# Gated attention plus MLP on one core: row-tiled scores, column-tiled PV on moving exponentials, a share of the exponentials on VectorE, and a list-scheduled engine order

## The chip, the cores and the metric

The kernel runs on one NeuronCore of one Trainium2 chip. The metric is the device time of one execution in microseconds (us). Each run is fast or slow (slow: more than 1.5% above the fastest of the same kernel); comparisons below use fast runs. The engines are named as in the profile: PE (TensorE matmuls), PEld (its weight loads), DVE (VectorE), ACT (ScalarE), POOL (GpSimd), SP (SyncE).

A profile is one execution taken by the hardware profiler. The trace behind it lists every instruction with its start and duration.

## The reference, cut to what matters

```python
def _A_ref(x, wqkv, wo):                       # x: 1 x 2048 x 640, bf16
    H = 32; Dh = 20
    qkv = (x @ wqkv) ...                       # q, k, v: 32 heads of 20 columns
    scores = einsum("bhqd,bhkd->bhqk", q, k) * Dh ** -0.5
    p = softmax(scores)                        # 32 x 2048 x 2048 exponentials
    o = einsum("bhqk,bhkd->bhqd", p, v)
    return o.reshape(B, S, D) @ wo

def _B_ref(x, w1, b1, w2):                     # F = 1536
    h = x @ w1 + b1
    act = h * tanh(softplus(h))                # mish
    return act @ w2

g = sigmoid((x * gate_w).sum(-1, keepdims=True))
return g * _A_ref(x, ...) + (1 - g) * _B_ref(x, ...)
```

The head dimension of 20 shapes everything: a score matmul uses 20 of the 128 rows of the PE array (in the trace its form is 20\*128, that of a projection 128\*128), and a PV product has only 21 useful columns (20 of V and a column of ones that sums the exponentials). The 134 million exponentials are the other large load.

## The kernel before

For each chunk of 512 queries and each group of two heads the kernel goes over 16 tiles of 128 keys. Two score matmuls fill a tile of 1024 columns in PSUM, ACT makes the exponentials, and eight matmuls with the *exponentials as weights* and V as the moving operand accumulate the output. Projections and MLP work are pumped in between on a credit count.

```python
for j in range(NS):                                   # 16 key tiles
    Sp = aps.tile([P, 2 * QC], F32, tag="S")
    for t in range(2):                                # two heads, two row strips
        nc.tensor.matmul(Sp[:, QC*t : QC*(t+1)],
            lhsT=kT_all[base+ROWB*t : base+ROWB*t+DH, p, j*P:(j+1)*P],
            rhs=qTc_p[base+ROWB*t : base+ROWB*t+DH, 0:QC],
            tile_position=(base + ROWB * t, 0))
    E = e_pool.tile([P, 2 * QC], BF16, tag="E")
    nc.scalar.activation(E, Sp, ACT.Exp, scale=inv_sqrt_dh)
    for t in range(2):
        for u in range(NU):                           # four blocks of 128 queries
            nc.tensor.matmul(acc[:, u, t, 0:DH+1],
                lhsT=E[:, QC*t + P*u : QC*t + P*(u+1)],   # exponentials as weights
                rhs=VA[:, j, h, 0:DH+1], ...)             # 21 moving columns
    pump_slot(slot_credit)                            # projections or MLP work
```

[... projections, mish by the identity (e^2+2e)/(e^2+2e+2) with a DVE reciprocal, output projection, and a transposing DMA of x at the start are cut ...]

The softmax here doesn't subtract the row's maximum and nothing guards it: scores larger than these inputs give would overflow.

## Time and profile before

| | before |
|---|---|
| time | 1387.95 us, median of 2 (1376.44 to 1399.46, the second 1.7% above the first and so slow by the rule above) |
| PE busy | 1235.3 us, 89% of the span |
| ACT busy | 1053.3 us, 76% |
| DVE busy | 463.9 us, 34% |
| mean granted PE clock | 0.608 of full |

The page's busy table, its slices (each digit is a fortieth of the span, in tenths busy; PEclk is the granted clock in tenths), and its chain of work that ended last:

```profile
PE 1235.3 (89%) x12384; PEld 589.6 (43%) x12384; DVE 463.9 (34%) x1093; ACT 1053.3 (76%) x1138; POOL 28.6 (2%) x51
...
PE   0699999988999988998889998998889988998887
...
ACT  0286666987768877698998777698998787699995
...
PEclk9975555975585555795555555695555555695555
...
PE 67%; ACT 25%; issue 3%; DMA 3%; DVE 1%; ACTq 0%
```

PE is nearly full while its clock is mostly at half, and the chain is two thirds PE.

Groups of instructions, by shape (out<-in, count | busy us, mean ns of one | idle just before them and what ended it):

```profile
L406 ACT ACTIVATE E<-Sp 128x1024 bf16<-128x1024 f32 x1024 | 1006.0, 1022 | 223.6 <-PE Sp L395 213.0 <-PE acc L412 0.9 <-ACT E L406 0.5
L395 PE MATMUL Sp<-qTc_p,kT_all 20*128 20x512 bf16 x2048 | 589.2, 559 | 0.0
L412 PE MATMUL acc<-VA,E 128*128 128x21 bf16 x8192 | 398.1, 182 | 95.5 <-ACT E L406 93.5 <-DVE O_qc L423 0.3
L412 PEld LDWEIGHTS <-E 128*128 128x128 bf16 x8192 | 335.7, 106 | 471.1 <-ACT E L406 376.9 <-issue 58.2 <-ACT e_sb L231 17.0
```

ACT lost 213.0 us waiting for scores. The 8192 small PV matmuls keep PE busy for 398.1 us and stream only 21 columns each.

### The profile page before, as it was taken

How to read it: one execution, taken by the hardware profiler on the slowest of the kernel's cores; microseconds unless marked ns; L12 is line 12 of the kernel's file. 1: busy time of each engine (PE TensorE's matmuls, PEld its weight loads, DVE VectorE, ACT ScalarE, POOL GpSimd, SP SyncE). 2: the span in 40 equal slices, each digit the busy share in tenths (PEclk: the TensorE clock that was granted, in tenths of full speed). 3: DMA queues.
4: the chain of work that ended last, by engine and by line, in shares of the span. 5: the costliest groups of instructions: out<-in, count | busy, mean ns of one | idle time of the engine just before them, and what ended most of it. 6: DMA issues, size and time to landing. Idle time of an engine off the chain costs nothing.

```text
span 1383.0 us, 28359 instructions
## 1 busy us (share of the span) xinstructions
PE 1235.3 (89%) x12384; PEld 589.6 (43%) x12384; DVE 463.9 (34%) x1093; ACT 1053.3 (76%) x1138; POOL 28.6 (2%) x51
## 2 busy tenths in 40 slices
PE   0699999988999988998889998998889988998887
PEld 0354444544444444443434444443434444453333
DVE  0222222377722576410101477410001476510002
ACT  0286666987768877698998777698998787699995
POOL 7000000000000000000000000000000000000000
PEclk9975555975585555795555555695555555695555
DMA  9600000000000000000000000000000000000000
GB/s 185 109 8 7 8 7 7 2 1 1 13 8 11 11 1 1 1 21 1 1 1 11 11 1 1 1 2 1 1 2 6 16 2 1 1 2 1 1 1 20
DMA packets 53086, 16.91 MB, mean 12 GB/s; under 512 B 49408, under 2 KB 52096, under 8 KB 52960
## 3 DMA queue, kind: packets, MB, share of 16 engines
q1 hardware_dynamic: 47456, 9.30, 4.6%
q0 software_dynamic: 912, 4.75, 1.2%
q10 hardware_dynamic: 4592, 1.03, 0.6%
q8 instruction: 97, 1.59, 0.5%
q14 instruction: 29, 0.24, 0.1%
HBM read 7.21 MB, written 2.62 MB: 7 GB/s over the span
## 4 chain that ended last, share of the span: by engine, by line
PE 67%; ACT 25%; issue 3%; DMA 3%; DVE 1%; ACTq 0%
PE Sp L395 26%; ACT E L406 25%; PE acc L412 15%; PE ph L223 8%; PE pk L143 5%; PE pb L261 4%; DMA xT<-in_A_x_dram 3%; PE pq L208 3%; PE pa L304 3%; PE pv L186 3%; PE pt L288 1%; ACTq L406 0%; PE pv L171 0%; ACT e_sb L231 0%; DVE d L311 0%
## 5 line engine op out<-in xcount | busy, mean ns | idle before, releaser
L406 ACT ACTIVATE E<-Sp 128x1024 bf16<-128x1024 f32 x1024 | 1006.0, 1022 | 223.6 <-PE Sp L395 213.0
L395 PE MATMUL Sp<-qTc_p,kT_all 20*128 20x512 bf16 x2048 | 589.2, 559 | 0.0
L412 PEld LDWEIGHTS <-E 128*128 128x128 bf16 x8192 | 335.7, 106 | 471.1 <-ACT E L406 376.9
L412 PE MATMUL acc<-VA,E 128*128 128x21 bf16 x8192 | 398.1, 182 | 95.5 <-ACT E L406 93.5
L241 DVE RECIPROCAL rd<-rd 128x256 f32<-128x256 f32 x96 | 167.4, 1744 | 0.8
L395 PEld LDWEIGHTS <-kT_all 20*128 20x128 bf16 x2048 | 104.3, 98 | 51.5 <-issue 18.2
L223 PE MATMUL ph<-xTc,w_sb 128*128 128x256 bf16 x480 | 119.0, 403 | 0.1
L421 DVE RECIPROCAL rden<-acc 128x8 f32<-128x8 f32 x64 | 12.4, 193 | 297.4 <-PE acc L412 297.4
L223 PEld LDWEIGHTS <-w_sb 128*128 128x128 bf16 x480 | 51.7, 128 | 57.4 <-issue 42.6
L234 DVE SCALAR_TENSOR_TENSOR e_sb<-e_sb 128x256 f32<-128x256 f32 x96 | 40.4, 421 | 100.5 <-ACT e_sb L231 99.6
L215 DVE CAST qTc_p<-pq 128x512 bf16<-128x512 f32 x32 | 22.1, 691 | 148.8 <-PE Sp L395 98.6
L231 ACT ACTIVATE e_sb<-ph,b1f 128x256 f32<-128x256 f32 x96 | 45.4, 473 | 33.8 <-PE ph L223 29.9
L143 PE MATMUL pk<-xT,wk 128*128 128x512 bf16 x140 | 66.0, 548 | 0.0
L208 PE MATMUL pq<-xTc,wqp 128*128 128x512 bf16 x160 | 64.5, 492 | 0.0
L261 PE MATMUL pb<-w_sb,actT 128*128 128x512 bf16 x192 | 58.0, 419 | 0.1
L150 DVE CAST kT_all<-pk 128x512 bf16<-128x512 f32 x32 | 22.1, 691 | 96.3 <-PE pk L143 96.3
L186 PE MATMUL pv<-wv,xT 128*128 128x80 bf16 x560 | 50.7, 237 | 0.0
L193 DVE CAST VA<-pv 128x80 bf16<-128x80 f32 x128 | 30.4, 243 | 57.7 <-PE pv L186 51.5
L143 PE MATMUL pk<-xT,wk_118 128*128 128x512 bf16 x20 | 7.2, 544 | 44.4 <-DMA xT<-in_A_x_dram 44.4
L243 DVE SCALAR_TENSOR_TENSOR actT<-ph,b1f,rd 128x256 bf16<-128x256 f32 x96 | 45.8, 478 | 0.1
L186 PEld LDWEIGHTS <-xT 128*128 128x128 bf16 x560 | 33.4, 117 | 23.2 <-issue 23.0
L261 PEld LDWEIGHTS <-actT 128*128 128x128 bf16 x384 | 28.5, 101 | 33.3 <-issue 24.1
(101 smaller groups left out, 351.9 us busy)
## 6 DMA issues: line engine op xcount, KB each, us to landing
w_sb<-in_B_w_dram POOLq DMA_DIRECT2D x2, 1920.0 KB, 31.1
out_dram<-ot SPq DMA_DIRECT2D x16, 160.0 KB, 1.8
Wq<-in_A_wqkv_dram ACTq DMA_DIRECT2D x1, 800.0 KB, 4.9
wo_sb<-in_A_wo_dram POOLq DMA_DIRECT2D x1, 800.0 KB, 24.5
wv<-in_A_wqkv_dram SPq DMA_DIRECT2D x7, 100.0 KB, 2.3
wk<-in_A_wqkv_dram SPq DMA_DIRECT2D x28, 25.0 KB, 2.6
wv_114<-in_A_wqkv_dram ACTq DMA_DIRECT2D x1, 100.0 KB, 10.7
wk_118<-in_A_wqkv_dram ACTq DMA_DIRECT2D x4, 25.0 KB, 29.7
```

The costliest lines, as they stand in the source:

```text
L143: nc.tensor.matmul(pk[:, 0:QC], lhsT=wk[:, kt, 0:P], rhs=xT[:, kt, sc * QC : (sc + 1) * QC], start=(kt == 0), stop=(kt == KT - 1),)
L186: nc.tensor.matmul(pv[:, 0 : 4 * DH], lhsT=lhsT, rhs=wv[:, kt, :], start=(kt == 0), stop=(kt == KT - 1),)
L208: nc.tensor.matmul(pq[:, 0:QC], lhsT=wqp[:, kt, p, 0:P], rhs=xTc[:, kt, 0:QC], start=(kt == 0), stop=(kt == KT - 1),)
L223: nc.tensor.matmul(ph[:, 0:CH], lhsT=w1_sb[:, kt, ft * P : (ft + 1) * P], rhs=xTc[:, kt, half * CH : (half + 1) * CH], start=(kt == 0), st ...
L231: nc.scalar.activation(e_sb, ph[:, 0:CH], ACT.Exp, bias=b1f[:, ft : ft + 1], scale=1.0)
L241: nc.vector.reciprocal(out=rd, in_=rd)
L243: nc.vector.scalar_tensor_tensor(out=actT[:, ft, half * CH : (half + 1) * CH], in0=ph[:, 0:CH], scalar=b1f[:, ft : ft + 1], in1=rd, op0=AL ...
L261: nc.tensor.matmul(tile_[:, 0 : col1 - col0], lhsT=actT[:, ft, u * P : (u + 1) * P], rhs=w2_sb[:, ft, col0:col1], start=(ft == 0), stop=(f ...
L304: nc.tensor.matmul(pa[:, :], lhsT=oT[:, ct, u * P : (u + 1) * P], rhs=wo_sb[:, ct, 0:CB], start=(ct == 0), stop=(ct == KT - 1),)
L395: nc.tensor.matmul(Sp[:, QC * t : QC * (t + 1)], lhsT=kT_all[base + ROWB * t : base + ROWB * t + DH, p, j * P : (j + 1) * P,], rhs=qTc_p[b ...
L406: nc.scalar.activation(E[:, :], Sp[:, :], ACT.Exp, scale=inv_sqrt_dh)
L412: nc.tensor.matmul(acc[:, u, t, 0 : DH + 1], lhsT=E[:, QC * t + P * u : QC * t + P * (u + 1)], rhs=VA[:, j, h, 0 : DH + 1], start=first, s ...
```

## The change

The intent has four parts. Scores: four heads of a group in four 32-row strips, two or three issued side by side. PV: V (with its ones column) becomes the *weights*, 32 columns wide, and the exponentials *move*, 512 at a time; four heads sit in four column strips of the array, so that one key tile of four heads is one bundle. Exponentials: for key tiles 6, 10 and 14 DVE makes them by bit fields, so ACT has 13 of 16. Order: every operation becomes a task with a cost, and a list scheduler written into the kernel fixes the order of each engine at build time. Mish moves to ACT (Exp, Ln, Tanh), x is transposed on PE, not by DMA, and the softmax normaliser goes through DRAM to be broadcast over partitions.

```diff
+DVE_KEYS = (6, 10, 14)
+ACT_KEYS = tuple(j for j in range(NS) if j not in DVE_KEYS)
+COEF = (0.458054, 0.465699, 0.0762946)
+SCALE = 0.5 / COEF[1]
+COEF = tuple(SCALE * c for c in COEF)
[...]
+class Order:                       # list scheduler: pick, for each engine, the task that
+    ...                            # can start first, by priority; for PE with look-ahead
[...]
+    for a, (G, j, r) in enumerate(blk):          # 3 or 2 blocks, by turns
+        nc.tensor.matmul(sb.tile[:, a*QC:(a+1)*QC],
+            lhsT=kt_all[32*r:32*r+32, G % NP, j*P:(j+1)*P],
+            rhs=q_buf[G].tile[32*r:32*r+32, :],
+            start=True, stop=True, tile_position=(32*r, 0))
+    nc.scalar.activation(eb.tile[:, 0:w], sb.tile[:, 0:w], ACT.Exp, bias=lnc, scale=inv)
[...]
+    for r in range(4):                           # PV: one bundle
+        ten, off = v_ap(j, 4*p + r, term)
+        nc.tensor.matmul(acc[32*r:32*r+32, :], lhsT=ten[:, off:off+32], rhs=srcs[r](),
+            start=k == 0, stop=k == pv_per - 1, tile_position=(0, 32*r))
[...]
+    # DVE's share: score * 128/ln2 + 127*128 written as uint16 is 2^n(1+f) as bf16 bits (e);
+    # n = e & 0xFF80;  m = (e & 0x7F) | 0x3F80;  m = m*m;  m = m*e
+    # the exponential is COEF[0]*n + COEF[1]*e + COEF[2]*m: three PV bundles with scaled V
+    nc.vector.tensor_scalar(out=e, in0=db.tile, scalar1=P*LOG2E*inv, scalar2=127.0*P,
+                            op0=ALU.mult, op1=ALU.add)
[...]
-    for j in range(NS):                          # the loop shown above, and the credit pump
[... 1259 lines of diff in all ...]
```

The bias `lnc` is the logarithm of SCALE. It scales ACT's exponentials so that COEF[1] can be exactly one half.

## The prediction

> **What bounds the kernel now.** TensorE, because its clock is low. The page's busy table has PE at 1235.3 us (89%), ACT 1053.3 (76%), DVE 463.9 (34%); the chain of waits is 67% PE, 25% ACT; the waits view has ACT idle 213.0 us for scores. The cores view gives a mean granted clock of 0.608. I replayed the matmul records in windows of 3.41 us and summed columns x rows/128 against the full-clock capacity. Of all windows that kept or won the full clock none used under 0.37, and those that lost it used 0.36 or less. Attention alone uses about 0.12 to 0.33 of the array, so the clock falls to half. [...] this trace shows only 1.0 and 0.5, in stretches of multiples of that.
>
> **What changes.**
> - Scores: still 2048 matmuls of 512 columns, but two or three 32-row strips at once, not two.
> - PV: 8192 matmuls of 21 columns (398.1 us busy, waiting 93.5 us for exponentials) and their 335.7 us of weight loads become 2816 of 512 columns, four column strips at once, with 32-column weights: 704 bundles of about 0.22 us at full clock (512-column durations less overlap), 0.43 at half.
> - ACT: 2048 blocks of 512 exponentials become 1664, in tiles of 1536 and 1024. Back to back, 128x1024 took 0.97 us in the timeline; from that and the slope I estimate 1.40 for 1536. 333 pairs: 789 us. Mish adds 36 activations of 2048 (estimate 1.82 each: 66 us) and 25 table loads at 1.283 (32 us). ACT about 890 us.
> - DVE takes 3 of 16 key tiles: 384 PSUM reads of 512 columns (0.691 each, as the casts now: 265 us), 192 bit-field passes and 384 multiplies of estimated 0.69 (forms scaled from 0.286, 0.419, 0.424 us): about 400 us. With evacuations 820 to 870 us. The mish reciprocal (167.4 us) and its companions go.
> - The DMA transposes go; PE now waits 44.4 us for the first. First exponential about 18 us after the start.
>
> **What then binds.** ACT first (890), DVE close (850), PE at full clock about 750 with switches between tilings. Per group of heads each needs 24 to 27 us. Weighted array use of the whole kernel is 1.17 M columns, 490 us at full clock: 0.5 of a 980 us span, above the 0.37 line, so I expect mean clock 0.80 to 0.95. In stretches without projections or MLP (about six of 32 groups, the last 2.6 above all) use is about 0.33, so the half clock returns and scores arrive late for ACT.
>
> **Sum.** 18 (head) + 890 (ACT) + 28 (tail: normalise through DRAM, output projection, store) + 50 (ACT waiting for scores) = 986, say **985 us, 80% range 940 to 1080**. Chances: faster by over 2% 0.97, within 2% 0.01, slower 0.02.
>
> **What would show it right or wrong.** ACT busiest, 88 to 92% of the span; 1536 tiles near 1.45 us mean; DVE 80 to 90%; chain of waits mostly ACT, PE behind; waits of ACT for scores under 80 us, mostly where the clock is half; DVE bit passes near 0.69 us.
>
> **What would make it wrong.** (a) A column-tiled bundle or a tiling switch costs more than estimated: PE leads again. (b) Four column strips count less for the clock, which stays at half: PE then needs about 1200 us, and the time goes to 1150 or more. (c) Bit passes at half the estimated rate (1.22 us) add 100 us to DVE, which then binds. (d) The static order drifts from real timings and engines stall in queue.

One clause about the clock is cut from the prediction: no trace of this case shows it. No term of the sum is touched: it is 18 + 890 + 28 + 50 = 986, as recorded. What the trace of the kernel before shows for the figures used in it:

- Its clock records hold only 1.0 and 0.5. All but the cut-off last one are whole multiples of 3.41 us long (6.83 us, the shortest, to 269.65 us); "that" in the prediction is these 3.41 us.
- Attention alone: from 622 to 720 us, with little else on PE, the clock was 0.50; the windows of the stretch from 605 to 741 us had a median use of 0.13.
- The full-clock capacity: at a clock of 1.00 successive 128x512 matmuls start 216 ns apart (median, L143 and L261), at 0.50 427 ns (L261). The 0.22 and 0.43 us of a bundle are estimates from these.
- The slope of ACT: 171 ns for 128x1 and 1022 ns for 128x1024, so 0.83 ns a column; with it the estimates of 1.40 and 1.82 us follow from 0.97.
- The 0.69 us of the bit passes is likewise an estimate: a f32 form of 128x256 took 0.419 us and of 128x512 0.691, a 16-bit copy of 128x512 0.424, the f32 TENSOR_SCALAR of 128x256 0.286. That the 16-bit passes gain over the f32 forms as the copy does was assumed.

## The result and the profile after

The changed kernel took 1039.33 us (1038.69 and 1039.97). The ratio, of fast runs compared round by round, is 0.7514 of before, 95% interval 0.7355 to 0.7673; the medians alone (the slow run with them) give 0.7488, the one fast run of the kernel before 0.755. Repeated in a later job it took 1040.15 us, 0.7501 (0.7443 to 0.7559).

The page's busy table, slices and chain, of the changed kernel:

```profile
PE 831.3 (80%) x6247; PEld 267.3 (26%) x6304; DVE 790.8 (76%) x1322; ACT 921.6 (89%) x731; POOL 35.3 (3%) x29
...
ACT  1757879998999999999999999999999999999991
...
PEclk9998999886696779997789989787989997599766
...
ACT 49%; PE 28%; issue 11%; DVE 7%; DMA 4%; SPq 1%; ACTq 0%; DVEq 0%
```

ACT leads now. Its digits are below 9 almost only in the first six slices. The mean granted clock is 0.859.

Groups by shape, changed kernel:

```profile
L597 ACT ACTIVATE E<-S,lnc 128x1536 bf16<-128x1536 f32 x333 | 523.0, 1571 | 27.7 <-PE S L579 19.3 <-PE X L634 8.2
L597 ACT ACTIVATE E<-S,lnc 128x1024 bf16<-128x1024 f32 x332 | 379.9, 1144 | 44.8 <-PE C L507 41.9 <-PE X L634 1.5 <-PE S L579 0.6
L646 DVE TENSOR_SCALAR e<-X 128x512 uint16<-128x512 f32 x384 | 260.8, 687 | 135.7 <-PE X L634 131.8 <-PE S L579 1.1
L663 DVE TENSOR_TENSOR m<-m 128x1024 bf16<-128x1024 bf16 x192 | 127.2, 683 | 0.3
L658 DVE TENSOR_SCALAR m<-e 128x2048 uint16<-128x2048 uint16 x96 | 66.2, 690 | 6.6 <-PE C L507 4.0
L745 ACT ACT_TABLE_LOAD x15 | 19.2, 1283 | 0.3
```

The same 128x1024 exponential that took 1022 ns now takes 1144. ACT waits little for scores (19.3 us before the wide tiles). Its largest wait, 41.9 us, is for PV (C): the ring of exponential tiles is full because PV has not read them yet. The DVE passes took 683 to 690 ns.

Stretches of the changed kernel (length, busy us of each engine with counts, granted clock, DMA). The cuts are the first exponential at 27.4 us and the end of the last at about 1015:

```profile
27.40:52.00 24.60, 21.29 (x204) 11.92 (x205) 15.84 (x48) 18.36 (x16) 8.62 (x15) 1.00 0.49 115
52.00:104.00 52.00, 47.89 (x320) 16.22 (x321) 46.28 (x87) 32.10 (x28) 0.00 (x0) 0.93 0.02 6
104.00:156.00 52.00, 45.94 (x339) 13.93 (x342) 47.17 (x79) 41.87 (x36) 0.00 (x0) 0.97 0.05 12
156.00:260.00 104.00, 84.67 (x644) 23.21 (x653) 87.82 (x145) 96.46 (x79) 0.00 (x0) 0.85 0.11 29
260.00:468.00 208.00, 171.45 (x1295) 53.71 (x1308) 162.93 (x266) 199.56 (x157) 0.00 (x0) 0.84 0.04 13
468.00:676.00 208.00, 165.93 (x1258) 52.98 (x1267) 158.63 (x259) 202.87 (x159) 0.00 (x0) 0.86 0.05 13
```

From 260 us on ACT (the fourth busy figure) is 96 to 98% busy. Between 27 and 156 us it is idle for 36.3 us (128.6 less 18.36, 32.10 and 41.87), while PE is about 90% busy (DVE too, from 52 us on) with the clock near full.

ACT's order of time shows the head and the largest hole (start us, us, what, [idle before]):

```profile
2.46 0.53 ACTq L288 DMA_DIRECT2D w2k<-in_A_wqkv_dram  x1
15.55 0.38 ACTq L288 DMA_DIRECT2D w2k<-in_gate_w_dram  x1
...
19.18 1.28 ACT L382 ACT_TABLE_LOAD   x1 [19.18 <-DMA w2k<-in_gate_w_dram]
...
27.40 1.54 ACT L597 ACTIVATE E<-S,lnc 128x1536 bf16<-128x1536 f32 x1 [3.85 <-PE S L579]
...
83.83 3.55 ACT L597 ACTIVATE E<-S,lnc 128x1024 bf16<-128x1024 f32 x3 [16.14 <-PE C L507]
```

ACT's own queue stands still from 3.0 to 15.6 us before it issues the next weight load; only at 19.2 us does it come to the copies of transposed x that the first scores need. At 67.7 us it stops for 16.14 us until PV has freed a buffer. What PV waits for stands in the order of time of PE and DVE:

```profile
81.39 0.68 DVE L668 TENSOR_TENSOR m<-m,e 128x1024 bf16<-128x1024 bf16 x1
82.13 0.40 PE L507 MATMUL C<-m,vd 128*32 128x512 bf16 x2 [1.02 <-DVE m L668]
82.60 0.68 DVE L690 COPY oraw<-C 128x512 f32<-128x512 f32 x1
83.33 0.74 PE L507 MATMUL C<-E,va 128*32 128x512 bf16 x8 [0.49 <-DVE oraw L690]
```

There is one accumulator C. The PV of the next group may not start before the last DVE key tile of the group before has been multiplied (L668), added to C, and C copied out (L690). So a late DVE pass holds up the PV of the tiles that ACT has finished, and with it ACT.

PE's order of time, a few lines of the steady state:

```profile
599.69 0.40 PE L579 MATMUL S<-q,kt_all 32*128 32x512 bf16 x3 [0.49 <-ACT E L597]
600.01 0.40 PE L507 MATMUL C<-E,va 128*32 128x512 bf16 x4
600.24 0.39 PE L507 MATMUL C<-m,vd 128*32 128x512 bf16 x4
600.56 0.31 PE L778 MATMUL X<-wo,arena 128*128 128x320 bf16 x1
```

Three score matmuls in three row strips, or four PV matmuls in four column strips, finish within 0.40 us together, at a clock of 1.00. A second bundle starts 0.23 us after the first; a matmul of another tiling starts 0.32 us after.

The sum that was predicted, beside what the profile shows:

| term | predicted | measured |
|---|---|---|
| until the first exponential | 18 | 27.4 |
| ACT busy from there | 890 | 918.7 (921.6 less 2.9 before) |
| ACT idle between first and last exponential | 50 | 69.4 (988.1 less 918.7): 36.3 before 156 us, 33.1 after |
| after the last exponential | 28 | 22.7 |
| span | 986 | 1038.2 |

### The profile page after: what moved, and what is told of

Same layout as the page of the kernel before. It is cut to its first block, busy times and chain, and to the rows that moved or that the text cites. A ratio compares the mean times of both kernels' runs of the same rounds, so it can differ in the third digit from the quotient of the medians.

```text
span 1038.2 us, 15472 instructions
## 1 busy us (share of the span) xinstructions
PE 831.3 (80%) x6247; PEld 267.3 (26%) x6304; DVE 790.8 (76%) x1322; ACT 921.6 (89%) x731; POOL 35.3 (3%) x29
## 4 chain that ended last, share of the span: by engine, by line
ACT 49%; PE 28%; issue 11%; DVE 7%; DMA 4%; SPq 1%; ACTq 0%; DVEq 0%
ACT E L597 40%; PE S L579 8%; PE C L507 7%; ACT arena L745 6%; PE X L763 3%; PE X L778 3%; PE X L427 2%; DVE e L646 2%; ACT L745 2%; PE X L439 2%; DMA rbc<-rows 2%; PE X L462 2%; PE X L727 1%; DMA w2k<-in_A_wqkv_dram 1%; ACT L597 1%
## 5 line engine op out<-in xcount | busy, mean ns | idle before, releaser
L597 ACT ACTIVATE E<-S,lnc 128x1536 bf16<-128x1536 f32 (+1 forms) x666 | 822.4, 1357 | 72.5 <-PE C L507 41.9
L579 PE MATMUL S<-q,kt_all 32*128 32x512 bf16 x1664 | 290.5, 428 | 146.1 <-ACT E L597 139.7
L646 DVE TENSOR_SCALAR e<-X 128x512 uint16<-128x512 f32 x384 | 260.8, 687 | 135.7 <-PE X L634 131.8
L507 PE MATMUL C<-E,va 128*32 128x512 bf16 x1664 | 183.3, 438 | 2.7 <-DVE oraw L690 1.5
L579 PEld LDWEIGHTS <-kt_all 32*128 32x128 bf16 x1664 | 83.4, 92 | 382.7 <-issue 375.6
L634 PE MATMUL X<-q,kt_all 32*128 32x512 bf16 x384 | 156.1, 428 | 3.6 <-DVE e L646 3.3
L663 DVE TENSOR_TENSOR m<-m 128x1024 bf16<-128x1024 bf16 x192 | 127.2, 683 | 0.3
L668 DVE TENSOR_TENSOR m<-m,e 128x1024 bf16<-128x1024 bf16 x192 | 126.6, 681 | 0.0
L727 PE MATMUL X<-xt,w 128*128 128x512 bf16 x219 | 70.5, 416 | 2.5 <-issue 1.7
L763 PE MATMUL X<-w2k,arena 128*128 128x320 bf16 x384 | 69.6, 305 | 0.7 <-DVE e L646 0.7
```

What stands on the lines that cost most here:

```text
L507: nc.tensor.matmul(acc[32 * r:32 * r + 32, :], lhsT=ten[:, off:off + 32], rhs=srcs[r](), start=k == 0, stop=k == pv_per - 1, tile_position ...
L579: nc.tensor.matmul(sb.tile[:, a * QC:(a + 1) * QC], lhsT=kt_all[32 * r:32 * r + 32, G % NP, j * P:(j + 1) * P], rhs=q_buf[G].tile[32 * r:3 ...
L597: nc.scalar.activation(eb.tile[:, 0:w], sb.tile[:, 0:w], ACT.Exp, bias=lnc, scale=inv)
L634: nc.tensor.matmul(db.tile[:, :], lhsT=kt_all[32 * r:32 * r + 32, G % NP, j * P:(j + 1) * P], rhs=q_buf[G].tile[32 * r:32 * r + 32, :], st ...
L646: nc.vector.tensor_scalar(out=vb_.tile[:, r * QC:(r + 1) * QC], in0=db.tile[:, :], scalar1=P * LOG2E * inv, scalar2=127.0 * P, op0=ALU.mul ...
L663: nc.vector.tensor_tensor(out=m, in0=m, in1=m, op=ALU.mult)
```

## The experiments

The kernel before is a poor yardstick between jobs: its median was between 1348.9 and 1396.1 us from one job to another. The changed kernel was steady (1037.4 to 1041.6 over six runs in two jobs). So its variants are compared by their own times; where they ran in different jobs, the text says so (the jobs ran on three chips, and the base of the later experiments and a variant that did not change the time agree over two of them: 1012.14 and 1012.59 us). All runs gave correct results.

### The yardstick, and ACT's bias operand (same job)

> The changed kernel once more, unaltered, as the yardstick for the runs beside it. Every theory expects 1036 to 1043 us, 0.75 of the kernel before.

It took 1040.15 us (1037.44 to 1041.62).

```diff
-SCALE = 0.5 / COEF[1]
-COEF = tuple(SCALE * c for c in COEF)
+SCALE = 1.0
-nc.scalar.activation(..., ACT.Exp, bias=lnc, scale=inv)
+nc.scalar.activation(..., ACT.Exp, scale=inv)
```

> The exponential of the ACT key tiles loses its per-partition bias operand (the VectorE polynomial then keeps its raw coefficients, so both halves still agree). Same engine order. Theory A: the bias operand costs about 76 ns of throughput per activation, because back to back the 128x1024 tile took 0.920 us before the change and 0.996 us after it. Then 128x1024 goes back to 0.92 us start to start, 128x1536 from 1.423 to 1.347, ACT is busy 50 us less (about 870) and the span falls to 990 to 1010 us. Rival B: the longer pitch comes from contention for PSUM or SBUF with the busier VectorE and TensorE; then the pitch stays 0.996 and the time 1039. Rival C: the pitch falls but ACT was not what bound the kernel; ACT busy falls 50 us, ACT idle grows by as much, the time stays within 10 us of 1039.

Measured: 1016.27 us (1012.43 to 1016.95), against 1040.15 beside it. Groups by shape of this run:

```profile
L596 ACT ACTIVATE E<-S 128x1536 bf16<-128x1536 f32 x333 | 486.8, 1462 | 44.8 <-PE S L578 28.0 <-PE X L633 14.8
L596 ACT ACTIVATE E<-S 128x1024 bf16<-128x1024 f32 x332 | 344.0, 1036 | 54.5 <-PE C L506 48.7 <-PE X L633 3.6 <-PE S L578 0.3
```

The mean fell from 1571 to 1462 and from 1144 to 1036 ns. From start to start, the median between consecutive ACT operations went from 1423 to 1346 ns and from 996 to 920 ns (the lower quartiles to 1330 and 903). ACT busy fell from 920.8 to 872.3 us. So the operand is a real cost, of the size that theory A gave, and B falls. But of the 48.5 us only 24 came off the span, where A expected 30 to 50: the idle before ACT's exponentials rose from 72.5 (27.7 and 44.8) to 99.3 us, so half of C holds as well. ACT leads, with PE and DVE close behind it.

By this run and the changed kernel, the operand cost 76 to 77 ns start to start by the medians, 92 to 93 by the lower quartiles, 108 to 109 in the mean duration.

### The head (same job as the yardstick)

```diff
-on_act = (c == 0 and i != 1) or (c == 1 and i == 1)
+on_act = False          # copies of transposed x on DVE
```

> The three copies of transposed x that ACT makes before the first exponentials go to VectorE, because ACT's own queue stands in a weight-load issue until 19 us (it waits 13 us for an earlier landing). Theory: the first exponential starts at 20 to 22 us instead of 27.4 and the time falls by 4 to 7 us, to 1032 to 1036. Rival: what is lost in the first 150 us is VectorE's and TensorE's backlog of K and V work, so that an earlier first exponential only waits longer later: first exponential earlier, time unchanged within 2 us.

Measured: 1034.08 us (1028.60 to 1038.61), 6 us less than the yardstick, with a spread of 10 us that overlaps it. The first exponential came at 24.1 us, not 20 to 22. ACT idle in the first 156 us fell only from 61.0 to 58.2 us. The direction is the theory's; the gain is not well resolved.

### No exponentials on DVE (same job)

```diff
-DVE_KEYS = (6, 10, 14)
+DVE_KEYS = ()
```

> No key tile on VectorE: all 16 on ACT, everything else as in the changed kernel. If ACT is what binds, its 2048 blocks cost 410 pairs of 2.42 us = 991 us instead of 805, so the time rises by about 150 to 186 us, to 1180 to 1225. VectorE busy falls from 791 to about 150. If instead PE (row and column tiling at the granted clock) or the static order binds, the time rises by less than 80 us, to under 1120, because PE also loses 384 score matmuls and 192 of 704 PV bundles.

Measured: 1259.42 us (1258.59 to 1262.98), 0.909 of before (0.902 to 0.916). ACT busy rose by 193 us to 1114.1 (89%), DVE fell to 204.0 us. The time rose by 219 us, more than either theory said: the mean clock fell to 0.716, and ACT's idle in half-clock stretches after 156 us grew from 22.4 to 73.9 us. Most of the whole gain hangs on the DVE share: without it the changed kernel is 127 us faster than before, with it 347 (medians, the kernel before by its fast runs alone: 1386.74).

In the early stretches, without DVE keys:

```profile
52.00:104.00 52.00, 51.69 (x327) 15.37 (x323) 18.39 (x29) 50.98 (x42) 0.00 (x0) 1.00 0.02 6
104.00:156.00 52.00, 43.58 (x260) 12.28 (x259) 10.36 (x16) 49.81 (x41) 0.00 (x0) 0.83 0.04 11
```

ACT's hole is gone (50.98 of 52 us busy, against 32.10). That points to the DVE keys as the cause of the early loss; the last experiment tests it.

### Was the kernel before slow because of its clock?

Two runs add useless matmuls to the kernel before: 168 moving columns against all-zero weights, accumulated into the same PSUM tile.

```diff
+            if j < NS - 1:
+                for _ in range(1):            # 4 in the second kernel
+                    nc.tensor.matmul(acc.rearrange("p u t d -> p (u t) d"),
+                        lhsT=zw[:, :], rhs=VA[:, j, 0:8, :], start=False, stop=False)
```

> The kernel before, with one matmul of 168 columns against all-zero 128x128 weights added to each key tile's accumulation (15 of 16 key tiles; it adds zero, so the result stays correct). Clock theory: the attention-only stages go from an array use of about 0.12 to 0.14 (0.13 + 0.07 at full clock's pace) to about 0.20 of full-clock capacity, still under the line of about 0.37 seen in the replay, so the clock stays at half there, the mean near 0.61, and the work is simply added where TensorE binds: 960 x 0.14 to 0.2 us, slower by 40 to 150 us (1430 to 1540). Rival (TensorE work alone counts, clock plays no part): also slower, by about 70 to 130 us.

> The kernel before, with four such zero matmuls per key tile. Clock theory: array use of the attention-only stages rises to 0.40 or more, above the line, so the clock stays at full nearly everywhere (mean 0.9 or more), TensorE then has slack, and the kernel gets faster although it does more: 1150 to 1280 us, ACT idle before its exponentials falls from 224 us to under 100. Rival (TensorE work alone counts): four times the cost of the run with one, slower by 280 to 500 us. If zero weights do not count for the clock, the rival's time with the clock near 0.6.

Measured: with one, 1449.4 us (median of three fast runs; a fourth was slow), 1.081 of before (1.066 to 1.096); with four, 1578.12 us, 1.168 (1.156 to 1.180). The second expectation failed: the mean clock rose only to 0.788 (the runs of the kernel before in this job had 0.618 to 0.638), ACT's idle for scores rose to 393.1 us instead of falling under 100, and the kernel got slower. Yet the stretches tell more than the total. The first 128 exponential tiles, while K, V and Q are projected, and then 64 tiles that stand nearly alone; first the kernel before (its one trace, from another job), then the kernel with one zero matmul:

```profile
64.30:154.20 89.90, 89.90 (x936) 44.79 (x933) 22.93 (x76) 63.51 (x64) 1.89 (x3) 0.61 0.08 7
154.20:253.40 99.20, 99.09 (x946) 46.04 (x946) 23.43 (x81) 64.82 (x64) 1.26 (x2) 0.54 0.06 6
605.50:673.40 67.90, 60.77 (x662) 26.86 (x662) 4.96 (x23) 62.22 (x66) 0.00 (x0) 0.58 0.05 11
```

```profile
63.00:137.00 74.00, 71.91 (x998) 38.91 (x997) 21.93 (x76) 63.42 (x65) 1.89 (x3) 1.00 0.10 9
137.00:213.10 76.10, 73.49 (x1006) 38.86 (x1004) 22.52 (x81) 63.42 (x65) 1.26 (x2) 1.00 0.08 9
606.40:678.00 71.60, 66.87 (x722) 28.43 (x722) 4.98 (x23) 64.08 (x64) 0.00 (x0) 0.61 0.05 11
```

Where K, V and Q are projected, the clock stayed at 1.00 with one more matmul per tile, and the same 128 tiles took 150.1 us instead of 189.1 (89.9 and 99.2): more work, less time. There, at 0.61 and 0.54 in the kernel before, the clock was the limit. That the added matmul alone held it is not shown: the runs of the kernel before differ in clock (0.584 to 0.641) and only one has a trace, so in its faster runs it may have held the clock there too. In the attention-only stretch the clock stayed low (0.58 and 0.61), and the work added 3.7 us to 67.9. There ACT was already 92% busy (62.22 of 67.90) at a clock of 0.58. Where MLP work began, the extra matmul did not lift the clock either: from the 257th to the 320th tile it was 0.50 in both kernels, and these 64 tiles took 103.2 us instead of 89.7.

The mean clock of the kernel with four stayed at 0.788. In the forecast I had worked out the use of the array at the pace of the full clock. The same attention-only work ran in both states, one after the other:

```profile
648.00:678.00 30.00, 29.49 (x387) 15.99 (x388) 2.74 (x12) 25.78 (x28) 0.00 (x0) 1.00 0.11 23
681.40:733.00 51.60, 51.28 (x488) 25.27 (x486) 2.83 (x12) 35.28 (x36) 0.00 (x0) 0.50 0.00 1
```

At a clock of 1.00 a tile took 1.07 us (28 in 30.00 us); at 0.50 it took 1.43 us (36 in 51.60 us), with PE busy 51.28 us of 51.60. From these times, and from the 512 columns in 216 ns that the trace of the kernel before shows at a clock of 1.00, I estimate that the tile's 1000 weighted columns (160 of scores, 168 of PV, 672 of zeros) come to 0.39 of full-clock capacity in the first stretch and to 0.30 in the second, on the two sides of the line of about 0.37. So at the slow pace the same work uses less of the array per unit of time. That this kept the clock at half, and what lost the full clock between the two stretches, was not shown. The added work has its own price too: the first 64 tiles, at a clock of 1.00 in both, took 90.9 us with four and 74.0 with one.

The line itself is what a replay of one trace, that of the kernel before, shows. Use: moving columns, times the share of the array's rows and columns that the weights fill, each matmul spread over its recorded duration, over the columns that the same trace streams at a clock of 1.00 (512 in 216 ns), in windows of 3.41 us from each change of the clock. The 72 windows that kept or won the full clock used 0.376 or more; of the 318 that lost it or stayed at half none used over 0.373. With each matmul counted where it starts, windows that kept it go down to 0.346, so the line is no sharper than that.

The matmuls against all-zero weights did raise the clock. The mean was 0.647 to 0.662 in the fast runs with one and 0.782 to 0.799 with four, against 0.618 to 0.638 in the runs of the kernel before in this job. In the first stretch above the clock was 1.00; without the zeros the tile's 328 columns would come to an estimated 0.13 there. In the kernel before, whose attention-only windows between 605 and 741 us had a median use of 0.13, it was 0.54.

### Both small edits, and K's copies on ACT (job of the two runs above)

> The changed kernel with both edits, no bias operand and the head's copies on VectorE. If the two gains are of different stages they add: 1040 - 24 - 6 to 11 = 1005 to 1011 us.

Measured: 1012.14 us (1008.55 to 1019.41). Against 1016.27 in the other job the step is inside the spread; the sum of the gains was not resolved. It serves as the base below.

```diff
 t_k[p, sc] = unit(KT, QC, mm,
-    lambda t: nc.vector.tensor_copy(out=kt_all[...], in_=t[:, 0:QC]), ...
+    lambda t: (nc.scalar.copy if p else nc.vector.tensor_copy)(out=kt_all[...], in_=t[:, 0:QC]),
+    ..., ev_eng="ACT" if p else "DVE")
```

> As the run with both edits, and the 28 evacuations of K for the head groups 1 to 7 move from VectorE (0.69 us each) to ACT (0.51 to 0.59 us each); the order is scheduled anew. Theory A: in the first eight groups VectorE binds (it is 90 to 97% busy between 52 and 170 us while ACT stands idle 30 to 35 us there), so relieving it of 19 us is worth 5 to 15 us although ACT gets 15 us more work: 992 to 1004 us. Rival B: TensorE's K and V projections or their place in the order bind there; then ACT's extra work is lost: 1012 to 1025 us.

Measured: 1021.02 us (1015.37 to 1025.08), 9 us slower by the medians, with ranges that overlap. ACT idle between 52 and 104 us did shrink, from 21.3 to 13.0 us, so DVE's load has a part in the hole, but ACT got 13.9 us more work (0.50 us for each of the 28 copies; of the expected 0.51 to 0.59, 0.59 is the 128x512 copy in the trace of the changed kernel) and the relief did not pay for it. The number is the rival's; the shrinking hole is not.

### Raising the clock of the changed kernel

```diff
+            if G in FILL and 0 < k < pv_per - 1:       # 14 of 32 head groups
+                for r in range(4):
+                    nc.tensor.matmul(acc[32*r:32*r+32, :], lhsT=zw[:, :], rhs=srcs[r](),
+                        start=False, stop=False, tile_position=(0, 32*r))
```

> As e4 (no bias, head's copies on VectorE), but in 14 of the 32 head groups, those that ran with little projection or MLP work beside them, each PV bundle but the first and last is followed by four column-strip matmuls against all-zero weights on the same moving tiles (280 bundles, about 0.22 us each at full clock; the result stays correct, the order of the rest is unchanged). Theory: the half clock costs ACT idle time there (32.5 us of it falls in half-clock stretches after 156 us); filling keeps use over the line of about 0.37, the mean clock rises from 0.86 to 0.93 or more, half-clock ACT idle falls to under 15 us and the time to 990 to 1002 us. Rival: as in the kernel with four zeros, the stretches that fall to half are too sparse to be lifted, the filler only delays scores: mean clock within 0.03 of 0.86 and 1012 to 1040 us.

Measured: 1029.29 us (1028.47 to 1032.92), in another job than the base's 1012.14: about 17 us slower, and as much above the variant below that ran in the same job (1012.59). Three thin stretches of the base:

```profile
312.00:390.00 78.00, 59.94 (x403) 16.37 (x402) 51.27 (x81) 71.73 (x58) 0.00 (x0) 0.69 0.03 8
468.00:546.00 78.00, 62.02 (x418) 17.47 (x417) 52.51 (x83) 72.11 (x59) 0.00 (x0) 0.73 0.03 8
650.00:728.00 78.00, 62.21 (x442) 17.64 (x439) 55.59 (x89) 72.72 (x59) 0.00 (x0) 0.76 0.03 8
```

The same stretches of time in the filled kernel:

```profile
312.00:390.00 78.00, 63.78 (x580) 18.97 (x579) 52.74 (x84) 69.86 (x57) 0.00 (x0) 0.86 0.03 8
468.00:546.00 78.00, 64.93 (x576) 19.08 (x576) 51.49 (x82) 71.17 (x58) 0.00 (x0) 0.81 0.03 8
650.00:728.00 78.00, 60.80 (x532) 17.20 (x531) 52.01 (x82) 70.72 (x57) 0.00 (x0) 0.80 0.03 8
```

The clock rose there from 0.73 to 0.82 in the mean (0.862 to 0.910 over all, between the two forecasts), and ACT did *less* in the same time: 211.8 us instead of 216.6. After 156 us its half-clock idle stayed (32.5 to 31.2 us), its full-clock idle rose from 24.8 to 40.3. That filling lifts the clock is so in this run; the theory's conclusion (the clock is worth the work) falls.

### Spreading V, and a plainer order (same job as the filled kernel)

```diff
-c0, hs0, nh = ((0, 0, 8), (161, 8, 24))[b]
+c0, hs0, nh = ((0, 0, 8), (161, 8, 12), (401, 20, 12))[b]
+        v_unit(2, j, at(3.2 + 0.1 * j), key=5)
```

> As e4, but V of heads 8 to 31 is projected in two parts: heads 8 to 19 when all were before, heads 20 to 31 two head groups later; the order is scheduled anew. Theory A: the ACT idle of about 38 us between the first exponential and 156 us comes from V work that is due at once in the first two groups (in the run of e4 PV waits up to 18 us and ACT with it, between 52 and 78 us ACT is busy 8 of 26 us). Then that hole shrinks to under 8 us, early idle falls by 10 us or more and the time to 995 to 1005 us. Rival B: TensorE and VectorE together are full in the first eight groups, so the hole only moves: early idle less, idle between 156 and 260 us more, time within 5 us of 1012.

Measured: 1012.59 us (1009.54 to 1015.11), no change. ACT idle between 104 and 156 us fell from 11.8 to 5.9 us and rose between 156 and 260 us from 10.5 to 15.7; between 52 and 104 us it stayed at 21.4. Spreading V alone moves the hole.

```diff
-                if t.prio == 0 or e + cost(t) <= lim + slack:
-                    pick = (e, t)
-                    break
+                pick = (e, t)
+                break
```

> As e4, but the list scheduler picks for TensorE simply the ready task of the best rank: the rules that hold back a long filler when a score tile is due soon, and that allow VectorE's scores only beside others, are gone. Theory: ACT runs out of scores more often (late ACT idle from 57 us to 90 us or more) and the time rises by 15 to 50 us, to 1027 to 1062. Rival: with two score tiles and five exponential tiles in flight the order hardly matters, within 6 us of 1012.

Measured: 1044.8 us (median of three fast runs, 1039.35 to 1048.53; a fourth was slow), some 33 us more than the base of the other job. ACT idle after 156 us rose from 57.3 to 78.9 us, not quite to the 90 expected; PE busy rose from 838.0 to 903.4 us. The look-ahead for due scores and the pairing of row strips, which fell together here, are worth about 3%.

### Fewer DVE keys at the start

```diff
+EARLY, EARLY_KEYS = 3, (10,)
+def dve_keys(G):
+    return EARLY_KEYS if G < EARLY else DVE_KEYS
+def act_keys(G):
+    return tuple(j for j in range(NS) if j not in dve_keys(G))
[... unscaled V of tiles 6 and 14 is kept for 12 heads as well; key lists by group ...]
```

> As e4, but the first three head groups give VectorE only one key tile of 16 instead of three (the other two tiles' V for those 12 heads is kept unscaled for ACT as well); the order is scheduled anew. Theory A: the hole in ACT between 52 and 156 us (33 us idle in e4, 3 us in the run without VectorE keys) comes from asking VectorE for three key tiles of bit-field work on top of the K and V evacuations of the start. Then that idle falls to under 15 us, ACT is busy 10 to 11 us more (24 blocks of 0.45 us), and the time falls to 994 to 1004 us. Rival B: TensorE's projections of K and V fill the start in any case, so the idle stays over 25 us and ACT's extra work is lost: 1012 to 1025 us.

Measured: 1003.88 us (1002.21 to 1005.46, six runs), 0.7331 of before (0.7290 to 0.7371). Two early stretches of the base (first fence) and of this kernel (second):

```profile
52.00:104.00 52.00, 48.20 (x319) 15.51 (x315) 47.11 (x80) 30.75 (x28) 0.00 (x0) 0.97 0.03 6
104.00:156.00 52.00, 46.92 (x343) 13.80 (x343) 47.90 (x81) 40.20 (x36) 0.00 (x0) 0.93 0.04 12
```

```profile
52.00:104.00 52.00, 51.85 (x346) 14.55 (x345) 33.04 (x55) 49.01 (x42) 0.00 (x0) 1.00 0.04 12
104.00:156.00 52.00, 49.30 (x359) 14.85 (x358) 40.87 (x70) 45.26 (x40) 0.00 (x0) 1.00 0.03 7
```

Idle of ACT in these 104 us fell from 33.1 (104 less 30.75 and 40.20) to 9.7 us, ACT busy rose over all by 10.8 us (869.6 to 880.4), and the time fell by 8 us against the base of the other job. PE is nearly full here in both, so what DVE lost was PE work too: a DVE key tile takes three PV bundles and separate score matmuls. Theory A holds in its numbers: too many DVE key tiles at the start made the hole, and the stop of 16 to 18 us is gone. How much of it was DVE's time and how much PE's was not separated. Of the 23 us of idle, ACT filled 10.8 with the exponentials it took over. Of all kernels run this is the fastest, 36 us below the changed kernel, and the two did not run in one job.

## Why the prediction was right or wrong

The time was right: 985 us predicted, range 940 to 1080, measured 1039.33. Faster by over 2% was given 0.97. But it was 5% low, and the sum shows where.

- **ACT binds next: right.** ACT is busy 89% (88 to 92% predicted) and leads the chain of waits with 49%, PE 28%.
- **"ACT about 890 us": 29 us too low.** I took 0.97 us for the 128x1024 tile from the kernel before and did not price the new bias operand. The mean of the 1536 tile was 1.57 us, not near 1.45. The run without the bias brings ACT to 872.3 us, below the 890: the 0.97 was itself about 0.05 too high (0.920 start to start, by the lower quartile), which hid a third of the operand's cost. That was luck.
- **"First exponential about 18 us after the start": 9 us too early.** It came at 27.4 us, after ACT's queue had been held by its own weight loads until 19.2 us. Taking ACT out of the head brought it to 24.1; why not to 18 stays open.
- **"50 (ACT waiting for scores) … mostly where the clock is half": wrong in place and cause, and 19 us too small.** The direct waits for scores were indeed small, but 36.3 of the 69.4 us of idle time lie before 156 us with the clock near full, where DVE key tiles, K and V all came due together and PV held the exponential buffers. The run with fewer early keys shows it: idle there from 33.1 to 9.7 us. Half-clock idle after 156 us was 23.8 us, and lifting the clock did not win it back.
- **Clock: right.** Mean 0.859 (0.80 to 0.95 predicted), with half-clock stretches where little projection or MLP work was at hand (from 264.6 to 285.1 us the clock was 0.50, with 4 projection matmuls beside 99 of scores and PV). Case (b), a clock that stays at half, did not come.
- **The line of 0.37: right as far as it goes,** which is the trace of the kernel before (0.376 or more against 0.373 or less). In the changed kernel the same replay is less clean: windows kept the full clock down to 0.33, two won it at 0.32, and one at 0.38 stayed at half (some matmul records are missing: 219 of 240 in one group). In the kernel with four zero matmuls the estimates of 0.39 at a clock of 1.00 and 0.30 at 0.50 agree with it. As a lever it did not pay: filling took 1029.29 us against 1012.14 and 1012.59.
- **"TensorE, because its clock is low": right for a part of the kernel.** At full clock, in the kernel with one zero matmul per tile, the projection stretch ran in 150.1 us instead of 189.1. In the attention-only stretch ACT was 92% busy even at a clock of 0.58.
- **PE about 750 us at full clock: not comparable as it stands.** It measured 831.3 at a clock of 0.859. The bundle was as estimated: two successive PV bundles start 0.23 us apart in the order of time (0.22 predicted). At full clock and back to back, a PV bundle starts 0.226 us after another (median), and a matmul of another tiling 0.333 us after a PV bundle (median). So a change between tilings cost about 0.1 us in this trace, which has 1487 of them: an estimate of 150 us of PE at full clock. The scheduler in the kernel reckons with 60 ns each, the author's estimate.
- **DVE bit passes 0.69 us: right** (0.683 to 0.690). DVE busy was 790.8 us, below the 820 to 870.
- **Tail: 22.7 us instead of 28.**

What stays open is how the remaining gap splits in the stretches after 156 us, where ACT is 96 to 98% busy and PE and DVE about 80%. And the runs did not undo row tiling or column tiling by itself; their share is seen only in the run without DVE keys, together with the new order.

## What to carry to other kernels

When three engines are balanced to within a fifth, add up the next engine's time with every operand of the new instruction form: a per-partition bias on 666 activations cost 48 us of ACT and 24 us of the kernel. A fixed share of work moved to a helper engine should follow the load of the stage: three key tiles of 16 were too many while K and V were being projected (no other number was tried later on). A low granted clock is a symptom to price by stage, with the idle time of the engine that binds there, before spending matmuls on lifting it.
